# A first MLP block computed tile by tile, and three side steps moved, in a fused attention and MLP kernel

## Chip, core and metric

The kernel runs on one core of one Trainium2 chip. The metric is the time of one launch on the device in microseconds (us), here the median of several runs. TensorE (PE) does matmuls and transposes into PSUM banks; VectorE (DVE) and ScalarE (ACT) empty those banks and do elementwise work; GpSimd (POOL) works on SBUF and issues casting loads; SyncE (SP) issues the other transfers. Each engine works through its own queue in order.

## The reference

For 8 batches of 8 heads, 576 tokens and head size 64, with a bias from the running sum of `max(s, 0)`:

```
scores = scale * q @ k.T + min(-(cum_i - cum_j), 0), causal
attn   = exp(scores - max) / (sum + 1e-9)
x      = heads of attn @ v side by side            # 576 x 512 per batch
xn     = (x - mean) / sqrt(var + 1e-6) * g_ln
out    = x + max(xn @ w_ch1, 0) @ w_ch2            # 512 -> 2048 -> 512
```

## The kernel before

The 64 (batch, head) pairs are 64 steps `n` of one hand-ordered loop (L732); `b, h = n // 8, n % 8`. The order of the Python statements is the order of each engine's queue, and PE takes up one step after the other. A step has these parts:

- `pre(n)` (L662) issues loads, some casts on POOL, and two fills of `cT`.
- `scores` (L300): three PSUM banks `sa`, `sb`, `sc` (pool `ps_s`, three banks), each followed by an exponential on ACT into `er` (L319). Up to step 9 the causal mask is a matmul as well (`NM`). `scores_d` (L337), in even steps after step 7, does the last 64 tokens of two heads in one bank of pool `ps_t`, tag "tr", which has two banks.
- `qk_pair(g)` (L271): transposes of one pair of heads of k and q (12 small matmuls, L251) into two banks (from g = 5 on of tag "tr"), then four copies into `kq`: k's two on DVE, q's two on ACT (L97, L99). `PAIRS` (L659) says at which step which pair is done: 9, 11, 13, 14, 15, 16 and 21. The scores of two heads read them later: pair 5 (step 9) is for steps 10 and 11, pair 7 (step 13) for 14 and 15. From batch 3 on DMA transposes do this work.
- `pv_next` (L717): the `pv` of the step two back (15 matmuls with a bank `pot`), its division on DVE into `xb` (and `xm` for the last 64 tokens), and after some heads the statistics of the norm (`ln_stats`, L419).
- `run_units` (L544): the MLP as a queue of units. `mlp1` (L480) makes one of 16 pieces `hT[:, fb]`: 4 matmuls of 512 columns and a ReLU on ACT, or on DVE for the first unit of a step. `mlp2` (L498) is a quarter of an output tile `py`, with the scaling by `rstd` and the residual on DVE after the fourth quarter (L511). 32 units make a batch.

The norm: `ln_xn` (L439) turns statistics into mean and variance (`bn_aggr`, L443) and makes `xn`, the centred tile times `g_ln`; `1/sqrt(var)` (`ln_rstd`, L433: an addition on DVE and a power on POOL) is only wanted by `mlp2`. `ln_tr` (L466) transposes a tile on PE and copies it to `xT` (L471, L97, L99). Batch 0 is special: its last `pv` is in step 7, its fourth tile is normed on POOL (L447, L450), and in step 8 all four tiles are transposed before the first `mlp1`. Batch 1's norm follows in steps 17 to 19, its MLP from step 20.

`bias_rows` (L221) transposes the running sums (15 matmuls into a "tr" bank `trc`) and copies them with four ACT copies to `cT`, which the row casts of batch 3 and later read.

Of the kernel before, what the change touches and what calls it, by code (L numbers as in the profile page):

```python
# [19 lines left out]
def kernel(  # L20
# [54 lines left out]
    hT = const.tile([P, FB, 512], BF16, name="hT")  # L75
    gb = const.tile([P, Dm], F32, name="gb")
    rstd = const.tile([P, B, NT], F32, name="rstd")
    mhalf = const.tile([P, 8], F32, name="mhalf")
    v_bf = [const.tile([P, NT, H, D + 1], BF16, name=f"v_bf{i}") for i in range(2)]

# [140 lines left out]
    def bias_rows():  # L221
        tr = ps_t.tile([P, 3, NT, BH], BF16, name="trc", tag="tr")
        for j, src in enumerate((c_hi, c_mid, c_lo)):
            for t in range(NT):
                pn = P if t < NF else TL
                nc.tensor.transpose(
                    tr[0:pn, j, t, :], src[:, t * P : t * P + pn], ident[0:BH, 0:BH]
                )
        for t0, t1, pn in ((0, NF, P), (NF, NT, TL)):
            nc.scalar.copy(  # L230
                out=cT[0:pn, t0:t1, 0, :, 1:4],
                in_=tr[0:pn, :, t0:t1, :].rearrange("p j t x -> p t x j"),
            )
            nc.scalar.copy(out=cT[0:pn, t0:t1, 1, :, 0], in_=tr[0:pn, 0, t0:t1, :])


    trs = {}
# [186 lines left out]
    xTs = {}  # L424
    xns = {}

    done = {}

    def ln_open(b):
        mvs[b] = small.tile([P, 5, 2], F32, name="mv", tag="mv", bufs=2)  # L430
        xTs[b] = xtp.tile([P, KD, 512], BF16, name="xT", tag="xT")
# [1 line left out]
    def ln_rstd(b):  # L433
        n = len(x_tiles(b))
        rs = rstd[:, b, 0:n]
        nc.vector.tensor_scalar_add(out=rs, in0=mvs[b][:, 0:n, 1], scalar1=1e-6)  # L436
        nc.gpsimd.tensor_tensor(out=rs, in0=rs, in1=mhalf[:, 0:n], op=ALU.pow)  # L437

    def ln_xn(b, t, on_pool=False):  # L439
        tiles = x_tiles(b)  # L440
        if t >= len(tiles):
            return
        nc.vector.bn_aggr(out=mvs[b][:, t, :], in_=st[b][:, t, 0 : 4 if b == 0 else 3, :])  # L443
        xn = xnp.tile([P, Dm], BF16, name="xn", tag="xn")
        if on_pool:
            xc = yop.tile([P, Dm], F32, name="xc", tag="yo")
            nc.gpsimd.tensor_scalar(  # L447
                out=xc, in0=tiles[t], scalar1=mvs[b][:, t, 0:1], scalar2=None, op0=ALU.subtract
            )
            nc.gpsimd.tensor_tensor(out=xn, in0=xc, in1=gb, op=ALU.mult)  # L450
        else:
            nc.vector.scalar_tensor_tensor(  # L452
                out=xn,
                in0=tiles[t],
                scalar=mvs[b][:, t, 0:1],
                in1=gb,
                op0=ALU.subtract,
                op1=ALU.mult,
            )
        xns[b, t] = xn  # L460
        done[b] = done.get(b, 0) + 1
        if done[b] == len(tiles):
            ln_rstd(b)

    def ln_tr(b, t, eng="dve"):
        if (b, t) not in xns:  # L466
            return
        xn = xns.pop((b, t))
        tr = ps_t.tile([P, KD, P], BF16, name="trx", tag="tr")
        for kd in range(KD):  # L470
            nc.tensor.transpose(tr[:, kd, :], xn[:, kd * P : (kd + 1) * P], ident)  # L471
        if t < NF:
            dst = xTs[b][:, :, t * P : (t + 1) * P]
        else:
            dst = xTm[:, :, (b // 2) * P : (b // 2 + 1) * P]
        copy_on(eng, dst, tr)
# [67 lines left out]
    def run_units(n, dve_first=False):  # L544
        for i in range(n):
            if queue:
                first_unit[0] = dve_first and i == 0
                queue.pop(0)()
# [3 lines left out]
    def keep_warm(n):  # L552
        w = ps_t.tile([P, 512], F32, name="idle", tag="tr")
        for _ in range(n):
            nc.tensor.matmul(w, lhsT=zeros[:, 0:P], rhs=zeros, start=True, stop=True)  # L555
# [106 lines left out]
    def pre(n):  # L662
        if n == 0:
            nc.vector.memset(mhalf, -0.5)
            ld_cast_pair(4)
        elif n == 1:
            ld_w1(1)
        elif n == 3:
            ld_cast_pair(5)
            for t in range(NT):  # L670
                ld_cast_v(1, t)
        elif n == 4:
            ld_w1(2)
            ld_w1(3)
        elif n == 8:
            ld_cast_pair(6)
            ld_w2(0)
            ld_cast_pair(7)
            ld_w2(1)
        elif n == 10:  # L680
            ld_w2(2)
            ld_w2(3)
        elif n == 12:
            bias_rows()
            nc.vector.memset(cT[:, :, 0, :, 0], -1.0)
            nc.vector.memset(cT[:, :, 1, :, 1:4], 1.0)
        elif n == 16:
            for r in rows:
                nc.gpsimd.memset(r[:, :, :, KA:P], 0.0)
        if n in PAIR_LOADS:  # L690
            ld_cast_pair(PAIR_LOADS[n])
        if n % 4 == 0 and 2 <= n // 4 + 1 < 2 * NPE:
            aug(n // 4 + 1, nc.sync)
        for gam in range(2 * NPE, NG):
            m = n - 4 * gam
            if m == -6:
                ld_rows(gam, 0), ld_rows(gam, 1)
            elif m == -5:
                cast_rows(gam, 0), cast_rows(gam, 1)
                ld_rows(gam, 2), ld_rows(gam, 3)  # L700
            elif m == -4:
                tr_rows(gam, 0), tr_rows(gam, 1)
                cast_rows(gam, 2), cast_rows(gam, 3)
                ld_rows(gam, 4)
            elif m == -3:
                tr_rows(gam, 2), tr_rows(gam, 3)
                cast_rows(gam, 4)
            elif m == -2:
                tr_rows(gam, 4)
        for nb in range(2, B):  # L710
            m = n - H * nb + (5 if nb == 2 else 7)
            if 0 <= m < NT:
                ld_v(nb, m)
            if 1 <= m <= NT:
                cast_v(nb, m - 1, "pool")

    def pv_next():  # L717
        pb, ph_ = pend.pop(0)
        pv(pb, ph_)
        if ph_ in (3, 5) or (ph_ == 7 and pb > 0):  # L720
            ln_stats(pb, ph_ // 2 - 1)
        elif pb == 0 and ph_ in (6, 7):
            ln_stats(0, ph_ - 4)
        if ph_ == 7:
            ln_open(pb)
            if pb == 0:
                ln_xn(0, 3, True)
            for t in range({0: 3, 1: 2, B - 1: 1}.get(pb, NT)):
                ln_xn(pb, t)


    for n in range(BH):  # L732
        b, h = n // H, n % H
        pre(n)
        if n < 8:
            scores(b, h)
            if h in (1, 3, 5, 6):
                scores_d(b, h // 2)
            if h in (0, 2, 4):
                qk_pair(h // 2 + 1, ("dve", "dve"), ("act", "dve" if h < 4 else "act"))  # L740
            pend.append((b, h))
            if n == 7:
                pv_next()
                tr_pair(4)
                pv_next()
                evac_pair("k", 4, ("act", "act"))
                evac_pair("q", 4, ("act", "act"))
                keep_warm(4)
                continue
            if n % 2 == 1 or n == 0:  # L750
                keep_warm(2)
            if n > 1:
                pv_next()
            if n == 6:
                pv_next()
            continue
        if n == 8:
            scores(b, h)
            scores_d(b, h // 2)
            pend.append((b, h))  # L760
            keep_warm(1)
            for t in range(NF):
                ln_tr(0, t, "act" if t < 3 else "dve")
            queue += batch_units(0)
            run_units(3)
            continue

        end = next(m for m in (8 * i + 3 for i in range(2, B + 1)) if m >= n)
        nu = (2 if n < 16 else -(-len(queue) // (end - n + 1))) - 2
        scores(b, h)  # L770
        run_units(1, True)
        if h % 2 == 0:
            scores_d(b, h // 2)
        run_units(1)
        if n in PAIRS:
            qk_pair(PAIRS[n], ("dve", "dve"), ("act", "act"))
        if n > 9:
            pv_next()
        pend.append((b, h))
        lt = {2: (0, 1), 3: (2, 3, 4)}.get(h, ()) if b > 1 else ()  # L780
        for t in lt:
            ln_tr(b - 1, t)
            if t != 1 and t != 4:
                run_units(1)
                nu -= 1
        if n == 2 * H + 2:
            for t in range(2, NT):
                ln_xn(1, t)
        run_units(nu)
        if b > 1 and h == 3:  # L790
            run_units(len(queue))
            queue += batch_units(b - 1)
# [41 lines left out]
```

## Time and profile before

| | |
|---|---|
| median of 6 runs | 378.38 us (377.73 to 379.95) |
| profiled execution | 378.07 us, of it the span from first to last instruction 376.3 us |
| PE busy | 359.2 us (95%), 2977 instructions |
| DVE, ACT, POOL busy | 205.2, 193.9, 166.2 us |
| `ph` matmuls (L484), `py` matmuls (L502) | 124.2 us, 134.1 us |
| chain that ended last: `ph`, `py` | 34%, 30% of the span |
| mean granted clock of TensorE | 0.982 |

The page splits the span into 40 slices of 9.4 us; each digit is a busy share in tenths, and PEclk is the clock granted to TensorE in tenths of full speed. A line of a timeline has start, duration, engine, source line, operation, the tile written and read, the count, and in brackets how long the engine had been idle before and what ended that. A line of the chain of waits has start, duration and what the end of the run waited for then. A line of the stretches view has the stretch, its length, the busy time of PE, weight loads, DVE, ACT and POOL, the granted clock as a fraction, the DMA share and GB/s. A busy PE is not PE at its peak.

### The profile page before, as it was taken

The page shows a single profiled execution, that of the slowest core. Times are in us where ns is not written, and L with a number is a line of the kernel's source. Part 1 is how long each engine was busy: PE and PEld are TensorE (multiplying, and loading weights), DVE is VectorE, ACT ScalarE, POOL GpSimd, SP SyncE. Part 2 cuts the span into 40 slices and gives each one's busy share as a digit, 9 for nine tenths or more (in the row PEclk, how much of TensorE's full clock was granted, in tenths as well). Part 3 has the DMA queues.
Part 4 walks back from the last instruction along what each step waited for, and adds up shares of the span by engine and source line. Part 5 has one row for each costly group of instructions (what it writes and reads, how often), then busy time and mean ns, then how long its engine had stood idle before and what let it go on. Part 6 is the DMA issues. An engine that isn't in the chain of part 4 may idle for free.

```text
span 376.3 us, 8216 instructions
## 1 busy us (share of the span) xinstructions
PE 359.2 (95%) x2977; PEld 198.0 (53%) x3028; DVE 205.2 (55%) x535; ACT 193.9 (52%) x371; POOL 166.2 (44%) x443
## 2 busy tenths in 40 slices
PE   8996888999999999999999999999999999999995
PEld 3673454655555555555555555555555554444444
DVE  7696265978636753684357545844485573212211
ACT  5895757843873377327732773277327713511410
POOL 8947346744572465536574565364652201000000
PEclk9997888999999999999999999999999999999999
DMA  8999998049994599749986999397930011002003
GB/s 146 171 185 169 168 162 139 4 89 225 194 194 119 134 229 195 181 119 230 185 193 169 206 208 180 79 238 174 205 99 28 2 50 64 1 30 84 0 30 85
DMA packets 147981, 50.42 MB, mean 134 GB/s; under 512 B 134185, under 2 KB 143268, under 8 KB 147940
## 3 DMA queue, kind: packets, MB, share of 16 engines
q1 hardware_dynamic: 129364, 40.74, 48.9%
q0 software_dynamic: 18176, 8.62, 19.3%
q10 hardware_dynamic: 400, 0.52, 0.5%
q8 instruction: 24, 0.39, 0.4%
q14 instruction: 17, 0.14, 0.2%
HBM read 37.11 MB, written 9.44 MB: 124 GB/s over the span
## 4 chain that ended last, share of the span: by engine, by line
PE 86%; DVE 7%; ACT 4%; issue 1%
PE ph L484 34%; PE py L502 30%; PE pot L385 7%; PE sa L308 3%; PE sc L308 3%; PE sb L308 3%; DVE xn L452 3%; PE trx L471 2%; ACT er L319 2%; ACT kq L97 2%; PE idle L555 2%; DVE stats L419 1%; PE trqk L251 1%; DVE xb L395 1%; DVE mv L443 1%
## 5 line engine op out<-in xcount | busy, mean ns | idle before, releaser
L502 PE MATMUL py<-w_bf,hT 128*128 128x512 bf16 (+1 forms) x570 | 134.1, 373 | 1.6 <-DVE yo L511 0.4
L484 PE MATMUL ph<-xT,w_bf 128*128 128x512 bf16 x488 | 124.2, 389 | 1.9 <-DVE xT L99 0.6
L494 ACT ACTIVATE hT<-ph 128x512 bf16<-128x512 f32 x105 | 62.7, 597 | 70.6 <-PE ph L484 70.6
L484 PEld LDWEIGHTS <-w_bf 128*128 128x128 bf16 x576 | 52.6, 99 | 56.0 <-issue 7.5
L502 PEld LDWEIGHTS <-hT 128*128 128x128 bf16 x592 | 53.5, 98 | 49.3 <-issue 0.9
L319 ACT ACTIVATE er<-sa 128x512 bf16<-128x512 f32 x64 | 38.1, 596 | 77.7 <-PE sa L308 49.4
L327 POOL TENSOR_SCALAR_AFFINE_SELECT er<-er 128x128 bf16<-128x128 bf16 x216 | 59.3, 298 | 35.0 <-ACT er L319 34.8
L492 DVE TENSOR_SCALAR hT<-ph 128x512 bf16<-128x512 f32 x39 | 27.0, 692 | 65.5 <-PE ph L484 59.1
L175 POOL CAST rows<-rowtmp 128x512 bf16<-128x512 f32 (+1 forms) x50 | 30.5, 610 | 45.3 <-DMA rowtmp<-in_q_dram 40.9
L308 PEld LDWEIGHTS <-kq 68*128 68x128 bf16 x440 | 32.9, 98 | 29.1 <-DVE kq L99 3.2
L385 PEld LDWEIGHTS <-er 128*128 128x128 bf16 x960 | 37.9, 99 | 13.4 <-issue 1.5
L385 PE MATMUL pot<-v_bf,er 128*128 128x65 bf16 x960 | 40.3, 195 | 0.3 <-PE sd L351 0.3
L393 DVE RECIPROCAL rinv<-pot 128x5 f32<-128x5 f32 x64 | 12.4, 193 | 51.5 <-PE pot L385 51.2
L319 ACT ACTIVATE er<-sc 128x512 bf16<-128x512 f32 x64 | 38.9, 608 | 0.0
L319 ACT ACTIVATE er<-sb 128x512 bf16<-128x512 f32 x64 | 38.2, 596 | 0.0
L511 DVE SCALAR_TENSOR_TENSOR yo<-py,rstd,xb 128x512 f32<-128x512 f32 x32 | 23.9, 748 | 23.9 <-PE py L502 16.5
L308 PE MATMUL sa<-kq 68*128 68x512 bf16 x64 | 24.4, 381 | 5.0 <-ACT kq L97 4.7
L395 DVE TENSOR_TENSOR xb<-pot,rinv 128x256 f32<-128x256 f32 x64 | 27.2, 425 | 2.2
L437 POOL TENSOR_TENSOR rstd<-rstd,mhalf 128x4 f32<-128x4 f32 (+1 forms) x8 | 8.8, 1098 | 40.2 <-DVE rstd L436 40.2
L101 POOL CAST v_bf<-vtmp 128x512 bf16<-128x512 f32 (+1 forms) x30 | 18.4, 615 | 18.0 <-DMA vtmp<-in_v_dram 17.9
L452 DVE SCALAR_TENSOR_TENSOR xn<-xb,mv,gb 128x512 bf16<-128x512 f32 x31 | 24.9, 804 | 1.1
L419 DVE BATCH_NORM_STATS2 stats<-xb 128x6 f32<-128x128 f32 (+2 forms) x100 | 25.3, 313 | 0.4
(95 smaller groups left out, 325.4 us busy)
## 6 DMA issues: line engine op xcount, KB each, us to landing
out_dram<-yo SPq DMA_DIRECT2D x32, 256.0 KB
vtmp<-in_v_dram SPq DMA_DIRECT2D x24, 256.0 KB
rowtmp<-in_k_dram SPq DMA_DIRECT2D x40, 128.0 KB
rowtmp<-in_q_dram SPq DMA_DIRECT2D x40, 128.0 KB
w_bf<-in_moe_w_ch_dram POOLq DMA_DIRECT2D x8, 512.0 KB, 10.0
kp<-in_k_dram POOLq DMA_DIRECT2D x11, 144.0 KB, 4.1
qp<-in_q_dram POOLq DMA_DIRECT2D x11, 144.0 KB, 4.8
v_bf<-in_v_dram POOLq DMA_DIRECT2D x8, 128.0 KB, 8.2
```

The source lines that it names most:

```text
L175: nc.gpsimd.tensor_copy(out=r[0:pn, :, :, 0:D], in_=loaded.pop(("rows", gam, t))[0:pn])
L308: nc.tensor.matmul(a[:, c + a0 - q0 : c + a1 - q0], lhsT=k_cols(b, h, kb), rhs=cols, start=True, stop=not (pe_mask and diag),)
L319: nc.scalar.activation(out=e[:, o : o + 512], in_=a, func=ACT.Exp, scale=scale)
L327: nc.gpsimd.affine_select(out=e[:, o : o + P], in_=e[:, o : o + P], compare_op=ALU.is_ge, fill=0.0, base=0, pattern=[[1, P]], channel_mult ...
L385: nc.tensor.matmul(pot[:, t, :], lhsT=e[:, o : o + P], rhs=vv[:, kb, h, :], start=(kb == 0), stop=(kb == last),)
L395: nc.vector.tensor_tensor(out=xb[b][:, :, hs], in0=pot[:, 0:NF, 0:D], in1=rinv[:, 0:NF].unsqueeze(2).to_broadcast([P, NF, D]), op=ALU.mult,)
L419: nc.vector.bn_stats(out=st[b][:, t, part, :], in_=x[:, lo:hi])
L452: nc.vector.scalar_tensor_tensor(out=xn, in0=tiles[t], scalar=mvs[b][:, t, 0:1], in1=gb, op0=ALU.subtract, op1=ALU.mult,)
L484: nc.tensor.matmul(ph, lhsT=w1_bf[:, kd, fb * P : (fb + 1) * P], rhs=xT[:, kd, :], start=(kd == 0), stop=(kd == KD - 1),)
L492: nc.vector.tensor_scalar_max(out=hT[:, fb, :], in0=ph, scalar1=0.0)
L494: nc.scalar.activation(out=hT[:, fb, :], in_=ph, func=ACT.Relu)
L502: nc.tensor.matmul(py[0], lhsT=hT[:, fb, t * P : (t + 1) * P], rhs=w2_bf[:, fb, c0:c1], start=(fb == 0), stop=(fb == FB - 1),)
```

## The change

Five things are done. In step 8 the first four `mlp1` pieces are computed column by column: after each tile's transposes, the 128 columns of the tile before it of all four pieces (16 matmuls of 128 columns), into two banks of `ps_m` and two of `ps_s`; the scores of step 8 follow these pieces, and one unit follows the scores (three before). The means of batch 0 come from the statistics in three small DVE steps for all four tiles at once (a product, a sum and a scaling), all four tiles are centred on DVE, and the variances with `rstd` follow after the four pieces. `qk_pair` stands ahead of its step's scores. `bias_rows` goes from the start of step 12 to the end of step 10, and its copies from ACT to DVE. The loads of pairs 6 and 7 and of half of `w_ch2` are issued in step 7 and not in step 8. The total number of units stays the same.

```diff
-            nc.scalar.copy(
+            nc.vector.tensor_copy(
                 out=cT[0:pn, t0:t1, 0, :, 1:4],
...
-            nc.scalar.copy(out=cT[0:pn, t0:t1, 1, :, 0], in_=tr[0:pn, 0, t0:t1, :])
+            nc.vector.tensor_copy(out=cT[0:pn, t0:t1, 1, :, 0], in_=tr[0:pn, 0, t0:t1, :])
...
+    def ln_aggr(b, t):
+        nc.vector.bn_aggr(out=mvs[b][:, t, :], in_=st[b][:, t, 0 : 4 if b == 0 else 3, :])
+
+    def ln_xn(b, t):
...
+        if b > 0:
+            ln_aggr(b, t)
...
+            scalar=mvs[b][:, t, 0:1] if b > 0 else mean0[:, t : t + 1],
...
+    def ln_first():
+        parts = st[0][:, 0:NF].rearrange("p t c (e x) -> p t (c e) x", x=3)
+        cm = small.tile([P, NF, 8], F32, name="cm", tag="cm", bufs=1)
+        nc.vector.tensor_tensor(out=cm, in0=parts[:, :, :, 0], in1=parts[:, :, :, 1], op=ALU.mult)
+        nc.vector.tensor_reduce(out=mean0, in_=cm, axis=AX.X, op=ALU.add)
+        nc.vector.tensor_scalar_mul(out=mean0, in0=mean0, scalar1=1.0 / Dm)
+        for t in range(NF):
+            ln_xn(0, t)
+
+    def ln_first_rstd():
+        for t in range(NF):
+            ln_aggr(0, t)
+        ln_rstd(0)
...
-        elif n == 8:
+        elif n == 7:
             ld_cast_pair(6)
             ld_w2(0)
             ld_cast_pair(7)
...
         elif n == 12:
-            bias_rows()
...
             if pb == 0:
-                ln_xn(0, 3, True)
-            for t in range({0: 3, 1: 2, B - 1: 1}.get(pb, NT)):
+                ln_first()
+                return
...
         if n == 8:
+            phs = [
+                pool.tile([P, 512], F32, name="ph", tag=tag)
+                for pool, tag in ((ps_m, "m"), (ps_m, "m"), (ps_s, "s"), (ps_s, "s"))
+            ]
+
+            def columns(t):
+                cols = slice(t * P, (t + 1) * P)
+                for fb, ph in enumerate(phs):
+                    for kd in range(KD):
+                        nc.tensor.matmul(
+                            ph[:, cols],
+                            lhsT=w1_bf[:, kd, fb * P : (fb + 1) * P],
+                            rhs=xTs[0][:, kd, cols],
+                            start=(kd == 0),
+                            stop=(kd == KD - 1),
+                        )
+
+            for t in range(NF):
+                ln_tr(0, t, "act" if t < 3 else "dve")
+                if t > 0:
+                    columns(t - 1)
+            columns(NF - 1)
+            for fb, ph in enumerate(phs):
+                if fb % 2 == 0:
+                    nc.scalar.activation(out=hT[:, fb, :], in_=ph, func=ACT.Relu)
+                else:
+                    nc.vector.tensor_scalar_max(out=hT[:, fb, :], in0=ph, scalar1=0.0)
+            ln_first_rstd()
+            queue += batch_units(0)[4:]
             scores(b, h)
             scores_d(b, h // 2)
             pend.append((b, h))
-            keep_warm(1)
-            for t in range(NF):
-                ln_tr(0, t, "act" if t < 3 else "dve")
-            queue += batch_units(0)
-            run_units(3)
+            run_units(1)
             continue
...
+        if n in PAIRS:
+            qk_pair(PAIRS[n], ("dve", "dve"), ("act", "act"))
         scores(b, h)
...
-        if n in PAIRS:
-            qk_pair(PAIRS[n], ("dve", "dve"), ("act", "act"))
         if n > 9:
             pv_next()
+        if n == 10:
+            bias_rows()
```

More of the change, by code (lines that the diff above doesn't have):

```diff
@@ L77 @@
     rstd = const.tile([P, B, NT], F32, name="rstd")
+    mean0 = const.tile([P, NF], F32, name="mean0")
     mhalf = const.tile([P, 8], F32, name="mhalf")
@@ L425 @@
     xns = {}
-    done = {}
     def ln_open(b):
@@ L437, in ln_rstd @@
         nc.gpsimd.tensor_tensor(out=rs, in0=rs, in1=mhalf[:, 0:n], op=ALU.pow)
-    def ln_xn(b, t, on_pool=False):
+    def ln_aggr(b, t):
+        nc.vector.bn_aggr(out=mvs[b][:, t, :], in_=st[b][:, t, 0 : 4 if b == 0 else 3, :])
+    def ln_xn(b, t):
         tiles = x_tiles(b)
@@ L442, in ln_xn @@
             return
-        nc.vector.bn_aggr(out=mvs[b][:, t, :], in_=st[b][:, t, 0 : 4 if b == 0 else 3, :])
+        if b > 0:
+            ln_aggr(b, t)
         xn = xnp.tile([P, Dm], BF16, name="xn", tag="xn")
[L445 to L459, printed above, removed]
+        nc.vector.scalar_tensor_tensor(
+            out=xn,
+            in0=tiles[t],
+            scalar=mvs[b][:, t, 0:1] if b > 0 else mean0[:, t : t + 1],
+            in1=gb,
+            op0=ALU.subtract,
+            op1=ALU.mult,
+        )
         xns[b, t] = xn
-        done[b] = done.get(b, 0) + 1
-        if done[b] == len(tiles):
+        if b > 0 and t == len(tiles) - 1:
             ln_rstd(b)
+    def ln_first():
[10 more added lines that the diff above has]
+        ln_rstd(0)
     def ln_tr(b, t, eng="dve"):
@@ L726, in pv_next @@
             if pb == 0:
-                ln_xn(0, 3, True)
-            for t in range({0: 3, 1: 2, B - 1: 1}.get(pb, NT)):
+                ln_first()
+                return
+            for t in range({1: 2, B - 1: 1}.get(pb, NT)):
                 ln_xn(pb, t)
@@ L757 @@
         if n == 8:
+            phs = [
[12 more added lines that the diff above has]
+                            stop=(kd == KD - 1),
+                        )
+            for t in range(NF):
[10 more added lines that the diff above has]
+            queue += batch_units(0)[4:]
             scores(b, h)
```

## Prediction

> **What bounds the kernel now.** I read the page first: busy slices, then the chain that ended last.
>
> ```profile
> span 376.3 us, 8216 instructions
> ...
> PE   8996888999999999999999999999999999999995
> ...
> PEclk9997888999999999999999999999999999999999
> ...
> PE 86%; DVE 7%; ACT 4%; issue 1%
> ```
>
> TensorE is full except in slices 3 and 5 to 7 (about 28 to 66 us), and only there is its clock below full. From 66 us on nothing but PE work can move the end, so the change, whose edits all lie between 26 and 92 us, is worth what it takes out of PE's path there. The engine's timeline in that stretch shows the waits (bracket: idle before, and what ended it):
>
> ```profile
> 30.23 0.38 PE L308 MATMUL sa<-kq 68*128 68x512 bf16 x1 [1.77 <-ACT kq L97]
> ...
> 44.97 0.38 PE L308 MATMUL sa<-kq 68*128 68x512 bf16 x1 [1.70 <-ACT kq L97]
> ...
> 54.27 1.14 PE L226 MATMUL trc<-ident,c 64*128 64x64 bf16 x15 [1.24 <-ACT kq L97]
> ...
> 64.65 0.38 PE L308 MATMUL sa<-kq 68*128 68x512 bf16 x1 [1.23 <-ACT kq L97]
> ```
>
> They are scores of step 8, 10 and 14, and the bias transposes of step 12; three of the four follow a `qk_pair` that stood at the end of the step before. Next the stretches view (length, busy time of PE, PEld, DVE, ACT, POOL, then the clock):
>
> ```profile
> 32.50:39.30 6.80, 5.34 (x21) 2.40 (x21) 1.88 (x3) 2.33 (x5) 6.09 (x9) 0.50 1.04 162
> 42.70:46.10 3.40, 1.70 (x21) 1.16 (x19) 1.58 (x2) 2.81 (x5) 0.05 (x1) 1.00 1.17 178
> 46.10:49.50 3.40, 3.40 (x24) 1.76 (x23) 0.69 (x1) 1.72 (x4) 1.37 (x5) 0.50 1.24 205
> ...
> 56.30:59.70 3.40, 3.40 (x19) 1.52 (x19) 1.15 (x2) 2.75 (x8) 1.60 (x6) 0.51 1.15 216
> 63.20:66.60 3.40, 2.12 (x20) 1.24 (x18) 3.26 (x9) 2.86 (x6) 1.72 (x4) 1.00 0.63 87
> ...
> 62.70:76.40 13.70, 12.08 (x150) 7.85 (x149) 13.17 (x29) 12.00 (x21) 9.48 (x25) 1.00 0.18 26
> ```
>
> After a stretch with 1.7 us idle (42.7 to 46.1) the next 3.4 us run at half clock; after 1.3 us idle (63.2 to 66.6) they don't. So a wait costs twice. The last line says that VectorE is nearly full from step 13 to 16 (13.17 of 13.70). The chain gives the PE prices, four matmuls of 512 columns at half and at full clock, and four transposes of 128:
>
> ```profile
> 47.16 1.71 PE ph L484 x4
> ...
> 66.39 0.86 PE ph L484 x4
> ...
> 84.63 0.22 PE trx L471 x4
> ```
>
> Full-clock prices of one step, from that view at 66 to 72 us: scores S 0.65 (0.9 with mask matmuls), MLP piece U 0.86, scores_d D 0.1, qk_pair transposes T 0.51, PV matmuls V 0.45; bias transposes 1.1.
>
> **The change, part by part.**
>
> *Step 8.* VectorE's last statistics end at 29.6 in both. Three tiny steps make the means: three times 0.16 (the 4-element L436) to 0.25 (L443); I take 0.6. POOL no longer streams, and the norm costs 0.75 as at 82.28 instead of the 1.18 and 1.46 beside POOL's L447 and L450. Tiles are ready at 31.0, 31.7, 32.4 and 33.1, the last at 33.9 before. PE, idle since 28.46, finds the clock falling at 32.5 as before. Transposes of tile 0 at 31.05, ScalarE copy 0.59, columns of tile 0 from 32.2. A 128-column matmul is new: full clock 0.055 (0.22/4 above) to 0.072 (the 15 bias transposes, 1.1/15), I take 0.06, since its shape is the transposes'; half clock 0.107 (1.71/16) to 0.131 (eight transposes in 1.05 at 33.94), I take 0.107. So tiles 0 and 1 with tile 2's transposes last until 35.9. That stretch is now full, so the clock returns at 35.9, not 39.3. Tile 3's transposes and 32 matmuls (2.0) end at 38.3. Scores of step 8 stand behind: two of their banks hold pieces that ScalarE and VectorE must empty (0.6 and 0.7 each), so `sc` starts near 39.3; then D and piece 5: step 9 begins at 40.6. Before it began at 39.8 with two pieces fewer (1.7): a gain of only 0.9.
>
> Here a rule speaks against the change. The Trainium skill (TensorE: Matmul & The Clock Gate, Back-to-back issue gap) gives about 81 ns per 128-column and 131 ns per 512-column matmul in a weights-and-matmul stream: 64 would cost 5.2 us against 2.1 for 16, 3.1 lost. The rows say 0.215 for 512 columns, so 64x0.06 = 3.8 against 3.4: 0.4 lost. I take the rows.
>
> *qk_pair ahead of scores.* Its evacuation (1.6 on each of ACT and DVE) now runs beside S and two U: the waits before steps 10 and 14 go (1.70 + 1.23). In exchange the exponentials stand behind it on ACT: step 9's last ends near 44.6, and the banks of step 10's scores wait 0.5. At step 14 VectorE first finishes PV's 0.98 and five statistics (1.7), then the key evacuation (1.62), and D needs one of only two "tr" banks. The trace shows no D waiting so. Counted from step 13's start, D of step 14 is due at 5.35. ACT ends its share at 6.1 (evacuation to 2.35, exponentials to 3.9, a piece to 4.5, evacuation 1.6); VectorE at 7.75 (V of 11 ends at 3.3, hand-over 0.15, then the three terms above). If D gets ACT's bank, it waits 0.75, at step 16 by the same count 0.35, and T 0.2 at 15: 1.3. If VectorE's, 2.4 and 1.9: 4.3. I take 1.3, because the nearest rows, the 1.24 wait at 54.27 and one at 74.56, end with ACT. The wait at 74.56 (0.28) goes.
>
> *bias_rows to step 10, copies to VectorE.* The 1.24 wait goes. But 15 transposes now end at 48.25, their copies follow on DVE, and step 11's `qk_pair` comes at once: its second transpose needs the bank that these copies free. DVE needs 1.0 (1280 elements at the rate of the `xT` copy, 512 in 0.41) to 1.8 (at that of `kq`'s strided copy, 576 in 0.81); I take 1.8, since these are strided too, and with the hand-over PE waits 1.7, and all behind it in its queue: S, both U and V of step 11. Cover for it: none.
>
> *Clock.* Of the half-clock stretches from 46.1 and 56.3, neither has its idle stretch any more: 2x1.7 = 3.4 gained. The Trainium skill (same page, Why this matters for your kernels) warns of PE gaps over about 3 us only; by it gaps of 1.2 to 1.8 cost no clock, their removal brings none, and I would say 377.2. The rows at 46.1 and 56.3 deny it here.
>
> *Steps 17 to 20.* Two pieces fewer are left for 17 to 19, but VectorE works from V of step 17 to the last copies of `xT` without a gap (80.0 to 91.9, 11.49 busy). One output step fewer in it leaves 11.1, PE needs 10.2: 0.9 lost.
>
> *At nothing.* POOL's loads of pairs 6, 7 and two of w2 move from 35 to about 27 to 33, past nothing but other issues there; used from step 11 on. The power on POOL and the variances (four L443, 0.16) fall in VectorE's idle 39 to 41; first used by `yo` at step 16. w2's other half is issued near 42, used from step 15; if the cover goes, each costs what it is late.
>
> Sum: 0.9 + 1.70 + 1.23 + 0.28 + 1.24 + 3.4 - 0.5 - 1.3 - 1.7 - 0.9 = 4.35. Laid out step by step at the prices above (step 11 at 48.25, 12 at 53.35, 13 at 56.35, 17 at 72.95, first piece of batch 1 at 87.05 against 91.9) it is 4.85. I take 4.6: the profiled 378.07 (span 376.3 and 1.8 around it) becomes 373.5, and the median of 378.38 becomes 373.8.
>
> **Rivals.**
> Hardly a new wait: DVE's copies and evacuations come in time, 1.7 and 1.3 go: 370.8. For it: VectorE has slack at steps 9 to 12. Against: two banks only.
> Clock again: 1.7 us idle around 49.5, beside slow transposes, drops it for 49.5 to 52.9 (half of the 2.65 us of work, 1.3), or a second stretch too (1.7): 375.1 to 376.8. For it: 52.9 to 56.3 held just that mixture and the clock fell.
> Key bank, on the slow side: D takes VectorE's bank at 14 and 16. 3.0 more waits, each about 2 us idle in one stretch, then two half-clock stretches (3.4): 380.2, slower; it decides from 5.7 us upward, so only with both clock drops. Against: ACT's bank is free sooner.
> Late loads: pairs 8 to 10 are now wanted 2.5 us earlier in their step, from 6 us after issue. They landed in 3.1 to 4.8 at 52 to 64 us; as slow as the slowest (10) the wait at step 14 is 5.5: 379.3.
> The column order does not do what it says: small matmuls keep the clock at half until 39.3, 32 of them 1.5 dearer: step 8 loses instead of gaining, 375.5.
>
> **How the numbers follow.** As summed 0.55 (371.5 to 376), hardly a new wait 0.13, clock again 0.12, column order 0.07, key bank 0.08, late loads 0.05. The range 370.3 to 377.6 leaves out the last two and some of the second. A measurement of this kernel can tell 0.3%, 1.1 us, from no change: faster 0.82, same 0.10, slower 0.08.
>
> **What would show it.** Right: no wait on `kq L97` in scores of steps 10 and 14; clock 1.00 from 36 us on; step 9 near 40.6; a PE wait of 1.5 to 2 us on `cT` copies of DVE in step 11; the first `ph` of batch 1 near 87. Wrong: D of steps 14 and 16 released by `kq L99`, PEclk of 0.5 after 40 us, or a transpose released by a `kp` or `qp` transfer.

## The result and the profile after

| | before | changed |
|---|---|---|
| median | 378.35 us (65 executions) | 377.16 us (28 executions, 373.05 to 380.13) |
| profiled execution | 378.07 us, span 376.3 | 374.36 us, span 372.6 |
| mean granted clock in it | 0.982 | 1.000 |
| PE busy | 359.2 us | 353.9 us |

The ratio to before is 0.9956, 95% interval 0.9938 to 0.9973: 1.2 us at the medians, where 4.6 was forecast. (The ratio leaves out executions over 1.5% above the fastest of their kernel and so isn't the ratio of these medians.) The profiled execution is not a typical one: it is 2.8 us below its own median, and its clock never fell. The page's lines that answer to those of before:

```profile
span 372.6 us, 8312 instructions
...
PE   8796978998999999999999999999999999999995
...
PEclk9999999999999999999999999999999999999999
...
PE 77%; DVE 9%; ACT 4%; DMA 4%; POOL 3%; issue 2%; ACTq 0%; POOLq 0%
```

Counted from 0, PE's gaps now lie, beside the start, in slices 1, 3, 5, 6 and 9; no edit lies before slice 2. PE's waits from 26 to 95 us (total, times, longest) show which are gone and which are new:

```profile
PE trx L481 <- DVE xn L448: 2.9, 2, 2.7
PE trqk L252 <- DVE cT L235: 1.8, 1, 1.8
PE trx L481 <- DVE xT L100: 1.0, 1, 1.0
PE trqk L252 <- DMA qp<-in_q_dram: 0.9, 1, 0.9
PE sd L344 <- ACT kq L98: 0.4, 2, 0.2
PE sb L309 <- ACT hT L793: 0.2, 1, 0.2
```

No first score (`sa`) waits for `kq L98` any more, only `sd` does, 0.2 us at a time. In their place stand one long wait for the first normed tile, one in step 11 for VectorE's bias copies, one in step 19 for an `xT` copy, and one for the late pair 8. All but the last are in the prediction's sum, the second with 1.7 us. What this profile can't show is why most executions take 377 and not 374 us. The clock of each execution is listed with its time, and in 51 executions of the changed kernel (with those of the first experiment) the two go together: median 373.7 us at a mean clock of 1.0 (2 of 51), 374.7 at 0.995 (17), 376.1 to 376.7 at 0.989 to 0.991 (5), 377.5 to 378.2 at 0.984 to 0.986 (18), and more at 0.981 or below (9). The kernel before has 374.55 us at 0.995 (10 of the 141 executions beside the experiments) and 378.6 at 0.982 (93 of them).

A stretch of 3.4 us at half clock takes 0.5x3.4/376 = 0.0045 from the mean clock, so 0.995, 0.991, 0.986 and 0.982 stand for one to four such stretches; the profile of before, at 0.982, has four (two from 32.5 to 39.3, then from 46.1 and from 56.3). At 0.995, the one value with more than a few executions of both kernels, they take the same time within 0.2 us. The changed one has a high clock more often: 24 of 51 executions have 0.989 or more, which is at most two such stretches; of before it is 13 of 141.

### The profile page after: what moved, and what is told of

Same layout as the page of the kernel before. It is cut to its first block, busy times and chain, and to the rows that moved or that the text cites. A ratio compares the mean times of both kernels' runs of the same rounds, so it can differ in the third digit from the quotient of the medians.

```text
span 372.6 us, 8312 instructions
## 1 busy us (share of the span) xinstructions
PE 353.9 (95%) x3025; PEld 197.4 (53%) x3075; DVE 207.3 (56%) x544; ACT 191.8 (51%) x366; POOL 164.2 (44%) x441
## 4 chain that ended last, share of the span: by engine, by line
PE 77%; DVE 9%; ACT 4%; DMA 4%; POOL 3%; issue 2%; ACTq 0%; POOLq 0%
PE ph L494 29%; PE py L512 28%; PE pot L386 6%; PE sc L309 3%; DVE xn L448 3%; PE sa L309 3%; PE sb L309 3%; ACT er L320 2%; DMA v_bf<-in_v_dram 2%; PE trx L481 2%; DMA qp<-in_q_dram 2%; ACT kq L98 1%; DVE stats L420 1%; DVE yo L521 1%; POOL v_bf L147 1%
## 5 line engine op out<-in xcount | busy, mean ns | idle before, releaser
L512 PE MATMUL py<-w_bf,hT 128*128 128x512 bf16 (+1 forms) x564 | 132.2, 373 | 1.6 <-DVE yo L521 0.4
L494 PE MATMUL ph<-xT,w_bf 128*128 128x512 bf16 x479 | 116.6, 379 | 1.2 <-DVE yo L521 0.2
L504 ACT ACTIVATE hT<-ph 128x512 bf16<-128x512 f32 x102 | 61.0, 598 | 63.5 <-PE ph L494 63.4
L494 PEld LDWEIGHTS <-w_bf 128*128 128x128 bf16 x560 | 50.3, 97 | 52.1 <-issue 3.6
L386 PEld LDWEIGHTS <-er 128*128 128x128 bf16 x960 | 37.5, 98 | 14.2 <-issue 0.7
L309 PE MATMUL sc<-kq 68*128 68x256 bf16 (+1 forms) x208 | 25.2, 232 | 0.3
```

The source lines that it names most:

```text
L309: nc.tensor.matmul(a[:, c + a0 - q0 : c + a1 - q0], lhsT=k_cols(b, h, kb), rhs=cols, start=True, stop=not (pe_mask and diag),)
L386: nc.tensor.matmul(pot[:, t, :], lhsT=e[:, o : o + P], rhs=vv[:, kb, h, :], start=(kb == 0), stop=(kb == last),)
L494: nc.tensor.matmul(ph, lhsT=w1_bf[:, kd, fb * P : (fb + 1) * P], rhs=xT[:, kd, :], start=(kd == 0), stop=(kd == KD - 1),)
L504: nc.scalar.activation(out=hT[:, fb, :], in_=ph, func=ACT.Relu)
L512: nc.tensor.matmul(py[0], lhsT=hT[:, fb, t * P : (t + 1) * P], rhs=w2_bf[:, fb, c0:c1], start=(fb == 0), stop=(fb == FB - 1),)
```

## The experiments

Medians, ratios to the kernel before on the same chip (95% interval), and in how many executions the mean clock was 0.989 or more (at most two stretches of 3.4 us at half clock). r1 to r4 share a chip, so do r5 to r8, r9 to r12, and r13 with r14. Times lie in groups by clock, so a median can jump from one group to the next; where a comparison rests on it, the means stand beside it.

| run | us | ratio | 0.989 or more |
|---|---|---|---|
| r1_again | 376.99 | 0.9957 (0.9927 to 0.9987) | 11 of 22 |
| r2_qk_only | 373.15 | 0.9884 (0.9837 to 0.9932) | 5 of 5 |
| r3_bias_late | 372.18 | 0.9864 (0.9807 to 0.9921) | 6 of 6 |
| r4_warm | 375.05 | 0.9913 (0.9891 to 0.9934) | 22 of 22 |
| r5_bias_act | 373.89 | 0.9884 (0.9859 to 0.9910) | 6 of 6 |
| r6_bias_at12 | 373.09 | 0.9857 (0.9840 to 0.9875) | 4 of 4 |
| r7_columns_only | 377.38 | 0.9948 (0.9923 to 0.9972) | 13 of 22 |
| r8_late_warm | 370.61 | 0.9788 (0.9774 to 0.9803) | 4 of 4 |
| r9_fill | 375.07 | 0.9938 (0.9914 to 0.9961) | 22 of 22 |
| r10_qk_warm | 372.32 | 0.9859 (0.9803 to 0.9914) | 5 of 6 |
| r11_at12_warm | 371.13 | 0.9845 (0.9788 to 0.9902) | 6 of 6 |
| r12_loads8 | 371.33 | 0.9838 (0.9786 to 0.9890) | 6 of 6 |
| r13_fill2 | 375.08 | 0.9912 (0.9887 to 0.9937) | 17 of 22 |
| r14_before_fill | 375.34 | 0.9944 (0.9915 to 0.9974) | 14 of 22 |

My theory: the waits went as forecast, and the clock did not stay. Its rival: new waits in other executions that one good profile doesn't show.

**The changed kernel again (r1_again).** No edit.

> The changed kernel once more, nothing altered, to see where the clock of TensorE falls in further executions. Theory 1 (clock): the waits went as forecast, but in most executions the clock still falls to half somewhere between 28 and 66 us, at places that differ from one execution to the next; the times then line up with the granted clock: about 374 us at a mean clock of 0.995 or more, about 378 us at 0.98 to 0.986. Theory 2 (waits): the profiled 374.36 us was lucky with its transfers; other executions show longer waits of PE between 30 and 92 us (a transpose on a late pair, V on a late load) at any clock, and the time does not follow the clock.

Its profiled execution (377.31 us, clock 0.984) is the typical one that was missing. The stretches view of it:

```profile
28.90:32.60 3.70, 0.92 (x11) 0.63 (x12) 3.56 (x13) 2.26 (x4) 1.88 (x3) 1.00 1.72 179
32.60:36.10 3.50, 3.50 (x36) 3.50 (x35) 0.74 (x2) 1.08 (x2) 0.92 (x2) 0.51 1.23 197
...
49.70:56.50 6.80, 6.02 (x35) 3.17 (x36) 2.78 (x6) 3.77 (x6) 2.64 (x7) 0.50 0.11 21
56.50:59.90 3.40, 3.40 (x46) 2.19 (x44) 2.51 (x6) 2.32 (x5) 2.29 (x7) 0.99 1.16 214
```

Half clock for 3.5 us after the wait for the first normed tile, as forecast, and again for 6.8 us from 49.7, while the wait of step 11 is still running. In the first profile the stretches around that wait stay at full clock:

```profile
46.30:49.70 3.40, 1.92 (x37) 1.44 (x33) 2.71 (x7) 0.60 (x1) 0.62 (x3) 1.00 1.18 198
49.70:56.50 6.80, 6.41 (x71) 3.93 (x73) 4.78 (x10) 5.81 (x11) 3.34 (x9) 1.00 0.40 82
```

PE's timeline there in r1_again:

```profile
47.18 1.16 PE L227 MATMUL trc<-ident,c 64*128 64x64 bf16 x15
48.27 0.43 PE L252 MATMUL trqk<-ident,kp 96*128 96x96 bf16 x6
50.48 0.64 PE L252 MATMUL trqk<-ident,qp 96*128 96x96 bf16 x6 [1.79 <-DVE cT L235]
50.91 0.63 PE L309 MATMUL sa<-kq 68*128 68x512 bf16 x1
51.34 0.63 PE L309 MATMUL sb<-kq 68*128 68x64 bf16 x2
51.77 0.63 PE L309 MATMUL sc<-kq 68*128 68x320 bf16 x2
52.19 3.62 PE L494 MATMUL ph<-xT,w_bf 128*128 128x512 bf16 x8
```

The second transpose has waited 1.79 us, as in the other profile (also 1.79); then eight matmuls take 3.62 us, where they take 1.89 at full clock. So both executions have the same wait there, and the clock makes the difference; the wait makes a fall likely and not certain.

**Head pairs ahead, alone (r2_qk_only).** On the kernel before:

```diff
+        if n in PAIRS:
+            qk_pair(PAIRS[n], ("dve", "dve"), ("act", "act"))
         scores(b, h)
...
-        if n in PAIRS:
-            qk_pair(PAIRS[n], ("dve", "dve"), ("act", "act"))
```

> The kernel before with one part of the change alone: the transposes and evacuations of a head pair ahead of their step's scores. Theory 1: the waits before steps 10 and 14 go (1.70 + 1.23 us), so two idle stretches fewer for the clock to fall after; 374 to 376.5 us. Theory 2: bias transposes at step 12 now wait for nothing either, but D waits at steps 14 and 16 come in; 375.5 to 378 us.

373.15 us, better than both theories said, and 3.8 us below the changed kernel, whose fastest of 22 executions here (373.91) is slower than the slowest of these five (373.88): this one edit is worth more than the whole change. The stretches after 46.1 and 56.3 of its profile, which were at half clock before:

```profile
46.10:49.50 3.40, 3.40 (x41) 2.15 (x40) 2.58 (x7) 2.81 (x6) 0.79 (x3) 1.00 1.24 204
56.30:59.70 3.40, 3.18 (x40) 2.06 (x39) 2.85 (x8) 3.34 (x6) 2.74 (x8) 1.00 1.33 201
```

(Step 8, from 32.3 to 39.3, is still at half clock in it.) Of the first scores' waits for `kq L97` only the one of step 8 is left:

```profile
PE sa L308 <- ACT kq L97: 1.8, 1, 1.8
```

The wait of the bias transposes at step 12 went too, although they stayed there; the banks of step 11's pair are empty by then, since the pair now comes ahead of the scores. That 1.24 us, which the prediction gave to the move of `bias_rows`, belongs to the pairs.

**Bias transposes to step 17 (r3_bias_late).**

```diff
-            nc.vector.tensor_copy(
+            nc.scalar.copy(
...
-        if n == 10:
+        if n == 17:
             bias_rows()
```

> The changed kernel with the bias transposes at the end of step 17 and their copies on ScalarE, so that no second transpose of step 11 waits for VectorE's copies (1.79 us idle of PE at 48.2 us in the profile of after). Theory 1: both that wait and the clock fall after it go: 1.8 us and up to 1.7 us, 373.5 to 375.5 us median. Theory 2: the wait alone goes, 375.4 us, less if VectorE is late elsewhere.

372.18 us: 4.8 below the changed kernel on the same chip, more than the wait and one 3.4 us stretch explain (1.8 + 1.7), and about what the wait and the two stretches behind it cost in r1_again (1.8 + 3.1). No execution of the six had a clock under 0.991.

**Idle matmuls in the wait of step 8 (r4_warm).**

```diff
-                keep_warm(4)
+                keep_warm(15)
                 continue
```

> The changed kernel with 15 instead of 4 idle matmuls at the end of step 7 (11 x 0.216 = 2.4 us in the 2.65 us that PE waits there for the first normed tile), which changes no wait. Theory 1: the clock no longer falls in step 8, the mean clock rises by 0.005 to 0.01 and the median falls by 1.5 to 3 us, to 374 to 375.7 us. Theory 2: no difference, 377.2 us (or 0.2 slower).

375.05 us, 1.9 below the changed kernel on the same chip (2.0 by the means), with no wait shortened on purpose; mean clock at least 0.989 in all 22 executions, as theory 1 said. Its profile (0.989) still falls to half clock from about 48.6 to 55.5 us, after the step 11 wait of 1.8 us: a count at 0.989 lets a fall of two stretches pass.

**Copies on ScalarE at the same place (r5_bias_act).**

```diff
-            nc.vector.tensor_copy(
+            nc.scalar.copy(
```

> The changed kernel with the four bias copies of step 10 on ScalarE, where they were, instead of VectorE. If the place is at fault (theory 1: whatever engine empties the bank, the next step's transposes want it at once), PE still waits 1.4 to 1.8 us in step 11 and the clock falls after it as often as before: 376 to 377.3 us. If VectorE is at fault (theory 2: its load delays the copies), the wait shrinks to under 0.5 us and the median is near 373.5 us.

Half a miss for each side. The wait is there, 1.5 us, as I said:

```profile
PE trqk L252 <- ACT cT L235: 1.5, 1, 1.5
```

but the median is 373.89 us and the mean clock was under 0.991 in none of the six executions. With a wait 0.3 us shorter the median is 3.1 us lower (another chip; 2.7 by the means). Whether the length or the engine does it, this run doesn't show; r13_fill2 below shortens the idle stretch behind VectorE's copies.

**Bias transposes back at step 12 (r6_bias_at12).**

```diff
         elif n == 12:
+            bias_rows()
...
-        if n == 10:
-            bias_rows()
```

with the copies on ScalarE as in the last diff.

> The changed kernel with the bias transposes back at the start of step 12 and their copies back on ScalarE; all else as changed. Theory 1: with the head pairs now ahead of the scores, step 12 has no pair before or after the transposes that contends for a bank: no wait, the clock stays after 40 us, 372 to 373.5 us. Theory 2: ScalarE's copies delay the exponentials of step 12 by 1.8 us and PE waits for them: 374.5 to 376 us.

373.09 us, no wait for a bias copy; theory 1. It is the changed kernel without the move of `bias_rows`, so that move, with its copies on VectorE, costs 3.9 us (377.0 against 373.1, on two chips). It is also the head pairs alone plus pieces by columns, means and loads: 373.09 against 373.15.

**Pieces by columns alone (r7_columns_only).** The changed kernel with `qk_pair` behind the units, `bias_rows` at step 12 on ScalarE and the loads in step 8, as before.

> The kernel before with the part that gives the change its name alone: the four pieces by columns and the means in one step; pairs, bias transposes and loads where they were before. Forecast from the prediction's sum for step 8: 0.9 us less than before in executions in which the clock falls in step 8, 377.5 us; the clock after 40 us stays as in before (half at 46 and 56 us). Rival: the 2.65 us that PE now waits in one piece for the first normed tile, and 64 small matmuls, cost as much as they bring: 378.2 to 379 us.

377.38 us against 378.57: 1.2 us, with 0.989 or more in 13 of 22 executions (1 of 27 of the kernel before beside it). The forecast of 0.9 was near, but executions at a mean clock of 0.995 take 374.8 us, like those of before (374.55): it is again the clock. And its profile (377.74 us, 0.991) denies half of what I expected of the clock: the wait of 1.70 us before step 10 is there, from 44.43 to 46.13, and no half clock follows it; the 1.25 us of step 12 are followed by one.

```profile
46.10:49.50 3.40, 3.37 (x34) 1.96 (x34) 0.93 (x3) 2.37 (x6) 1.38 (x5) 1.00 1.22 198
56.30:59.70 3.40, 3.40 (x26) 1.75 (x24) 0.91 (x3) 2.59 (x8) 2.08 (x7) 0.51 0.99 184
```

**Both idle stretches gone (r8_late_warm).** r3 with the edit of r4.

> The changed kernel with the bias transposes at the end of step 17 (copies on ScalarE), and 15 instead of 4 idle matmuls at the end of step 7. With both idle stretches gone after which the clock was seen to fall (at 32 and at 49 us) it should stay at 0.998 or more in nearly all executions: 370.2 to 371.5 us. Rival: the clock falls elsewhere (waits of 0.6 us for a pair, 0.3 for VectorE), mean 0.991 to 0.995, 372 us as without the idle matmuls.

370.61 us (370.15 to 370.85), ratio 0.9788 (0.9774 to 0.9803), clock 1.0 in every execution; the lines of the profiled one:

```profile
span 368.4 us, 8384 instructions
...
PE   8999999999999999999999999999999999999995
```

It beats both kernels, and its four executions lie within 0.7 us, where the changed kernel's 28 spread over 7.1.

**The wait of step 11 filled (r9_fill).** On the changed kernel:

```diff
     def qk_pair(g, k_engs, q_engs):
-        tr_pair(g)
+        tr_kind("k", g)
+        if g == 6:
+            w = ps_o.tile([P, 512], F32, name="fill", tag="pot")
+            for _ in range(8):
+                nc.tensor.matmul(w, lhsT=zeros[:, 0:P], rhs=zeros, start=True, stop=True)
+        tr_kind("q", g)
```

> The changed kernel with 8 idle matmuls (8 x 0.216 = 1.73 us) between the two transposes of step 11, in the bank of PV, which is free then: they fill the 1.79 us in which the second transpose waits for VectorE's copies and change no wait. If the clock, and not the wait, makes most of the difference between the copies on VectorE (377 us) and on ScalarE (373.9 us): the clock no longer falls at 49 us, mean clock 0.995 in nearly all executions, 374.2 to 375 us. If the copies on VectorE cost through the waits behind them (later evacuations, later statistics): no change, 376.5 to 377.2 us.

375.07 us, mean clock 0.989 or more in 22 of 22. PE gets to the second transpose at the same distance from the first (50.77 to 52.99):

```profile
50.77 0.43 PE L252 MATMUL trqk<-ident,kp 96*128 96x96 bf16 x6
51.03 1.89 PE L277 MATMUL fill<-zeros 128*128 128x512 bf16 x7
52.99 0.41 PE L252 MATMUL trqk<-ident,qp 96*128 96x96 bf16 x6
```

2.2 us from transpose to transpose with the fill, 2.2 without it (48.27 to 50.48 in r1_again): the distance is the same, and what the fill brings is the clock behind it. (One of the eight matmuls is missing from the trace.) It is 1.9 us of the median and 1.5 of the mean (376.8 over the 51 executions to 375.3). As ratios to before beside it, 0.9957 and 0.9938, the two intervals overlap; the clock tells them apart better: below 0.989 in 27 of 51 executions without the fill, in none of 22 with it.

The profiled execution, at 377.15 us, lost its clock elsewhere, from 14.2 to 21.0 us, ahead of all that was edited, when a score had waited 1.81 us for a transfer; its step 11 begins at 50.77 us, for 48.27 in r1_again:

```profile
14.17 0.61 PE L314 MATMUL sa<-kq 68*128 68x512 bf16 x1 [1.81 <-DMA kq<-c]
14.20:21.00 6.80, 6.80 (x55) 4.73 (x55) 1.64 (x3) 4.42 (x8) 4.45 (x6) 0.50 1.37 206
```

That wait is none in some profiles, 0.6 us in r1_again, 1.5 in the first one and 2.1 in r10_qk_warm, and half clock followed it in the three profiles in which it was 1.6 us or more (r9, r10, r13) and in no other. None of the experiments holds it fixed, so the rival, waits that differ between executions, is true of this one place and part of the scatter.

**A part of it filled (r13_fill2).** The same with `range(2)`.

> The changed kernel with 2 idle matmuls (0.43 us) instead of 8 between the two transposes of step 11, which leaves about 1.4 us idle there, as long as the wait behind ScalarE's copies (1.49). If the length of the idle stretch decides whether the clock falls: it mostly holds as with 8, 374.2 to 375.5 us, mean clock 0.991 or more in most executions. If something else in VectorE's copies decides: 376.3 to 377.3 us as without idle matmuls.

375.08 us (mean 375.4), 0.989 or more in 17 of 22. With 1.79 us idle it is 24 of 51, with about 1.4 it is 17 of 22, with none 22 of 22. Length counts, as far as runs on three chips can tell, and doesn't decide alone: the profile of this run is one of the other five (379.51 us, 0.981), with half clock behind this shortened wait too.

**The wait of the kernel before filled (r14_before_fill).**

```diff
+        if n == 10:
+            w = ps_o.tile([P, 512], F32, name="fill", tag="pot")
+            for _ in range(7):
+                nc.tensor.matmul(w, lhsT=zeros[:, 0:P], rhs=zeros, start=True, stop=True)
         scores(b, h)
         run_units(1, True)
```

> The kernel before with 7 idle matmuls (1.5 us) in the 1.70 us that PE waits ahead of step 10's scores, in the bank of PV; the wait is unchanged. If the clock is what waits cost twice: no half clock from 46.1 to 49.5, mean clock 0.986 instead of 0.982, 1 to 1.7 us less than before, 376.7 to 377.5 us. If the clock falls there for another reason: 378.3 to 378.6 us.

375.34 us against 378.9 beside it, more than expected, from seven matmuls that compute nothing. By the means it is less, 376.7 against 378.9: 2.2 us, where the change brings 1.7 to 1.8. The stretches that follow the waits (half clock before):

```profile
46.00:49.40 3.40, 3.35 (x33) 1.90 (x33) 1.60 (x4) 2.81 (x7) 1.53 (x6) 1.00 1.23 203
56.20:59.60 3.40, 3.40 (x38) 2.04 (x37) 1.83 (x5) 3.28 (x9) 2.84 (x8) 1.00 0.79 155
```

The wait of step 12 (1.2 us) is still in this profile, yet 56.2 to 59.6 is at full clock too.

**Pieces by columns at a held clock (r10_qk_warm, r11_at12_warm).** r10 is r2 with `keep_warm(12)` in place of 4 at the end of step 7; r11 is r6 with the edit of r4.

> The kernel before with the head pairs ahead of the scores and with 12 instead of 4 idle matmuls at the end of step 7 (8 x 0.216 = 1.73 us in the 1.77 us that PE waits there); no pieces by columns. If the pieces by columns are worth something at a held clock: the three further waits of step 8 remain (0.5 + 0.8 + 0.6), 371.8 to 373 us, and the clock may fall after them at 35.7. If they are worth nothing: 371 us, as with them.

> The changed kernel with the bias transposes back at the start of step 12 (copies on ScalarE) and 15 idle matmuls at the end of step 7; it differs from the one with the head pairs and idle matmuls alone by the pieces by columns, the means in one step and the earlier loads. Worth something: 370.8 to 371.6 us, 1 us or more below that kernel. Worth nothing: within 0.4 us of it.

372.32 against 371.13 us on one chip, but r10's six spread from 370.93 to 377.31 with the clock. Its two executions at 0.998 and 1.0 take 370.93 and 371.45, beside r11's 370.59 to 371.33 at 0.998 or more. So the pieces by columns save little or nothing by themselves at a held clock, as far as two executions can tell; whether they make the clock steadier, six executions of each don't show.

**Loads back in step 8 (r12_loads8).** r8 with `elif n == 8` for the loads.

> The changed kernel with the bias transposes at the end of step 17 and 15 idle matmuls (370.6 us, clock 1.0), with the loads of pairs 6 and 7 and of half of w2 issued in step 8 again. The prediction counted their move at nothing: 370.3 to 370.9 us. Rival: in step 8 POOL issues them after the power for the scaling at 39 us, pair 6 lands after step 11 begins, and PE waits for it 1 us or more: 371.5 us or above.

371.33 us (370.01 to 372.13), between the two expectations and on another chip than r8; no wait for pair 6 in its profile. The move is worth too little to be told apart here.

## Why the prediction was wrong, step by step

Starts of PE's work in us, counted as the prediction laid them out (its steps assume the clock at half from 32.5 to 35.9 only):

| | forecast | profile, clock 1.0 | r1_again, 0.984 |
|---|---|---|---|
| step 9 | 40.6 | 40.15 | 40.63 |
| step 10 | 43.7 | 43.28 | 43.76 |
| step 11 | 48.25 | 47.79 | 48.27 |
| step 12 | 53.35 | 53.10 | 56.45 |
| step 13 | 56.35 | 56.19 | 59.38 |
| step 17 | 72.95 | 73.58 | 76.36 |
| first piece of batch 1 | 87.05 | 87.81 | 90.76 |

Up to step 11 the layout holds within 0.02 us in the typical execution. Then 3.1 us are lost in one step, and 3.7 stand at the end.

- **The step that failed is the clock.** The sum took "2x1.7 = 3.4 gained", since "neither has its idle stretch any more", right after it had put a new idle stretch of 1.7 us into step 11. The price of that stretch by the prediction's own rule, that a wait costs twice, was left out of the sum and given to a rival of chance 0.12: 1.3 us for one stretch of 3.4, or 3.0 with a second. It was 3.1 in r1_again, where the clock stayed low for 6.8 us, and 0.5 after 40 us was one of the prediction's own signs of being wrong. So that rival is what happened in the typical execution. The 4.85 of the layout less the 3.7 at its end is 1.15, and 1.2 was measured. Why two stretches is not shown; the first of them began with 0.8 us idle.
- **The rule itself was too firm.** It came from one execution of before, in which 2.11 us busy from 52.9 to 56.3 lost the clock and 2.12 from 63.2 kept it. The same wait of 1.79 us cost no clock in the first profile, nor did 1.70 us in r7's; a wait of this length makes a fall likely, and the sum needed it as a share of executions.
- **The wait itself was right**: 1.79 us for 1.7. So were the copies on VectorE, from 47.90 to 49.86 (1.96 for 1.8).
- **Step 8**: the first transpose came 2.6 us after the last idle matmul, as laid out (28.46 to 31.05). Sixteen 128-column matmuls took 1.05 us, about 0.055 each behind the first's latency, for 0.06. The Trainium skill's 81 ns, and 131 for 512 columns, did not hold; the rows did. By r7's median the step's gain is 1.2, for 0.9.

```profile
33.63 1.05 PE L778 MATMUL ph<-xT,w_bf 128*128 128x128 bf16 x16
34.52 0.39 PE L481 MATMUL trx<-ident,xn 128*128 128x128 bf16 x4
```

- **Head pairs**: the waits before steps 10 and 14 are gone. D of steps 14 and 16 gets ScalarE's bank and waits 0.2 us each (0.4 in r1_again for one), for 0.75 and 0.35; VectorE's bank, the slower rival, did not come.
- **Credited to the wrong edit**: the 1.24 us of step 12 are the pairs' doing (r2). With that, moving `bias_rows` had only a cost, and the prediction's sum should have had it as 1.7 and a fallen clock for nothing.
- **Late loads**: pair 8 was 0.9 us late in the profiled execution and not in r1_again; 5.5 was far too much.
- **Steps 17 to 20**: the wait for the `xT` copy is 1.0 and 1.2 us, for 0.9.
- **At nothing**: loads and variances cost nothing that shows.
- **A reading**: the slices "3 and 5 to 7" are 3 to 6, counted from 0; the times given with them are right.

Compared at 0.995, before and changed take 374.55 and 374.7 us. The prediction's sum without its clock term was 0.95 us, and the 0.9 of step 8 in it counts on the clock too (back at 35.9 and not at 39.3), so it leaves little for an equal clock. That fits: nearly the whole effect that can be seen of this change is how often the clock is held.

## To carry to other kernels

On an engine whose clock follows its activity, as TensorE's did here when idle matmuls filled its waits, each wait that an edit adds is priced with the clock behind it, just as each wait that it removes, and what removal credits to the clock is taken back where the same edit makes a new hole. Credit a removed wait to the one edit that removes it, and then ask what the other edits do alone: here one moved line was worth more than the whole change, and another took most of it away. Where the clock differs from execution to execution, one profile is one draw; read the listed clocks before the trace.

## What the hardware showed that I had not expected

Seven or eight matmuls of zeros, put into waits that stayed as long as they were, took 1.5 us (r9_fill) and 2.2 us (r14_before_fill) off the means, 1.9 and 3.6 off the medians. The half clock comes in pieces of 3.4 and 6.8 us, and the same kernel has a mean clock from 0.972 to 1.0 in different executions; the Trainium skill (TensorE: Matmul & The Clock Gate, What's actually happening) says that the activity window of about 3.4 us runs freely and isn't reset by the kernel, which fits. It doesn't fit that only gaps over about 3 us should matter: here waits of 1.2 to 1.8 us were enough in many executions, beside transposes (the 15 bias transposes take 1.16 us of PE for 64 columns each). Which share of activity in a window keeps the clock stays open: 1.70 us busy of 3.40 lost it and 2.12 kept it in the kernel before, yet 2.11 of 3.40 from 52.9 to 56.3 lost it, with those transposes among them; in r7's profile 1.73 from 42.7 to 46.1 kept it and 2.51 from 52.9 to 56.3, transposes again, lost it. Where a wait falls in the window, and what a transpose counts there, would have to be varied alone.
